# The third pair's k and q loaded earlier and transposed by DMA from ScalarE's queue, in a fused retention and bilinear-FFN kernel

## The chip, the cores and the metric

The kernel runs on one core of a Trainium2 chip. The metric is the device time of one execution in microseconds. The five engines of a core run their own instruction queues: TensorE (PE, with weight loads shown apart as PEld), VectorE (DVE), ScalarE (ACT), GpSimd (POOL), and SyncE (SP), which here only issues transfers. Sixteen DMA engines move the data.

## The reference

Inputs are q, k, v of shape (4, 8, 768, 64), that is batch, heads, sequence and head size, and three weights w_a, w_b (512 x 1536) and w_out (1536 x 512). All of them are float32.

```python
for t in range(S):                       # per batch and head, gamma = 1 - 2^(-5-h)
    state = gamma * state + outer(k[t], v[t])
    y[t] = scale * q[t] @ state
x = y.transpose(0, 2, 1, 3).reshape(B * S, H * D)     # 3072 tokens x 512
out = ((x @ w_a) * (x @ w_b)) @ w_out
```

## The kernel before, in words

The sequence is cut into 24 chunks of 128 rows, called slots 0 to 23, six for each batch entry. The recurrence is computed by chunks: inside a chunk by a masked matrix of scores k.q, between chunks by a running state. The decay is folded into k and q when they are scaled by a table and turned to bf16 (`scaled`, line 212; the result is `kqb`, with k and q side by side).

The FFN works on token tiles; `TILES` says how many slots each of the eight tiles has. The first tile has four slots (512 tokens). For each of twelve blocks `ft` of 128 hidden columns, `ffn_a` (line 504) makes `a` with four matmuls, which ScalarE copies to bf16 (line 508), and `ffn_g` (line 516) makes `g`, which VectorE multiplies with that copy (line 519). `parts` splits a block's matmuls into two halves of columns where it says so. When all twelve blocks are done, `ffn_out` (line 544) multiplies by w_out.

Slots 0 to 5 go by pairs (a pair `u` is slots 2u and 2u+1, loaded by `load_pair` in one transfer each for k, q and v). Their k and q have to be transposed before the scores: `flip2` does that on TensorE against an identity (line 395), into PSUM, and ScalarE or VectorE copies the result to SBUF (`kT2`, `qT2`). Pairs 0 and 1 run at the start, since they feed the first FFN tile; pair 2, the third one, is worked in between the blocks of the first tile. From slot 6 on, `casts` scales a slot on POOL and transposes it with a DMA that SP issues (`dma_start_transpose`, line 225); `turn` later runs its states and scores.

The order of work is written out by hand. `seq` chains every instruction of an engine to the one before it, so each engine runs in the order in which the code is written. `LOADS` is the order of SP's first transfers: k, q, v by pair, `w0` to `w5` (a sixth of w_a and of w_b each), `o0` to `o5` (w_out) and `s6`, `s7` (the loads of slots 6 and 7). POOL turns weights to bf16 (`cast_w`, `cast_o`, line 184). Blocks 2j and 2j+1 use the weights of `w`j.

Around the change the written order of TensorE is: blocks 2 to 7 in pairs (a, a, g, g), block 8, the transposes of the third pair's k, a of block 9, the transposes of its q, g of block 9, the scores of both slots (`scores2`, line 408), the first state update (`update2`, line 431), a of blocks 10 and 11, g of block 10, `intra2` and `inter2` (lines 460 and 448), g of block 11, the second tile's twelve blocks, and then the output matmuls, with `turn(6, None)` ahead of the second output row block and `turn(8, 6)` some 11 us later. PSUM has three rotating banks for `a`, `g`, `tp` and half of the scores (pool `psff`); the staging buffers of weights rotate by four, so `o4` and `o5` reuse those of `w4`.

Of the kernel before, what the change touches and what calls it, by code (L numbers as in the profile page):

```python
# [10 lines left out]
BF16 = mybir.dt.bfloat16  # L11
# [5 lines left out]
PAIRS = 3  # L17


LOADS = "k0 q0 k1 q1 v0 v1 w0 w1 w2 w3 w4 k2 q2 v2 w5 o0 o1 o2 o3 o4 o5 s6 s7".split()  # L20


@with_exitstack
def kernel(
# [10 lines left out]
    nc = tc.nc  # L35
    P = 128
    B, H, S, D = q.shape
    NCH = S // P
    HP = H // 2
# [3 lines left out]
    NFT = DFF // P  # L43
    NSLOT = B * NCH
    NW = 6
    WC = DFF // NW
    FPW = NFT // NW
# [11 lines left out]
    tra = ctx.enter_context(tc.tile_pool(name="tra", bufs=4))  # L59
# [22 lines left out]
    def load_slot(t, names="kqv"):  # L82
        b, ci = divmod(t, NCH)
        for nm in names:
            if t % 2 == 0:
                whole[nm] = raw.tile([P, 2, H, D], F32, tag=nm + "f", name=nm + "f")
            raws[nm, t] = whole[nm][:, t % 2]
            s = {"k": k, "q": q, "v": v}[nm][b, :, ci * P : (ci + 1) * P, :]
            seq(nc.sync.dma_start(out=raws[nm, t], in_=s.rearrange("h p d -> p h d")))
# [21 lines left out]

    pending = list(LOADS)

# [9 lines left out]
    kqb = {}  # L123
# [52 lines left out]
    wa_bf = wpool.tile([P, KT, DFF], BF16, name="wa_bf")  # L176
    wb_bf = wpool.tile([P, KT, DFF], BF16, name="wb_bf")
    wo_bf = wpool.tile([P, NFT, DM], BF16, name="wo_bf")

    def cast(engine, dst, src):  # L180
        if engine is nc.scalar:
            seq(nc.scalar.copy(dst, src))  # L182
        else:
            seq(engine.tensor_copy(dst, src))  # L184

    def cast_w(j, parts=1):
        for nm, dst in (("a", wa_bf), ("b", wb_bf)):
            for x in range(parts):
                a, b = x * WC // parts, (x + 1) * WC // parts
                cast(nc.gpsimd, dst[:, :, j * WC + a : j * WC + b], wst[nm, j][:, :, a:b])  # L190
# [15 lines left out]
    def scaled(eng, t, i):  # L206
        ktab, qtab = tabs[0] if t < 2 * PAIRS else tabs[1]
        dst, src, tab = kqb[t][:, i], raws["kq"[i], t], (ktab, qtab)[i][:, t % NCH]
        dst = dst.rearrange("p hp r d -> p r hp d")
        src = src.rearrange("p (r hp) d -> p r hp d", r=2)  # L210
        tab = tab.rearrange("p (r hp) o -> p r hp o", r=2).to_broadcast([P, 2, HP, D])
        seq(eng.tensor_tensor(dst, src, tab, op=ALU.mult))  # L212

    def new_nat(t):
        kqb[t] = nat.tile([P, 2, HP, 2, D], BF16, tag="kqb", name="kqb")
        kb[t], qb[t] = kqb[t][:, 0], kqb[t][:, 1]
        vb[t] = nat.tile([P, H, D], BF16, tag="vb", name="vb")

    def casts(t, names="kqv"):
        if "k" in names:  # L220
            new_nat(t)
            scaled(nc.gpsimd, t, 0)
            scaled(nc.gpsimd, t, 1)
            kqT[t] = tra.tile([P, 2, HP, P], BF16, tag="kqT", name="kqT", bufs=6)
            seq(nc.sync.dma_start_transpose(
                out=kqT[t].rearrange("p a b c -> p (a b) c"),
                in_=kqb[t].rearrange("p a hp r d -> p (a hp r d)")))
            if t % 2 and t + 1 < NSLOT:
                for names in ("kq", "v"):
                    load_slot(t + 1, names)  # L230
                    load_slot(t + 2, names)
        if "v" in names:
            cast(nc.gpsimd, vb[t], raws["v", t])

    def half(i):
        return slice(64 * i, 64 * i + 64)
# [52 lines left out]

    ys, begun = {}, set()  # L290

    after = mybir.DependencyInfo(mybir.DependencyClass.Sync, mybir.DependencyReason.DATA)
    mark = lgr[:, 0, :1]
    fence = {}

# [75 lines left out]
                later.append(lambda c=c: leave(old, c, apart))  # L371


    kT2, qT2, ats = {}, {}, {}
# [12 lines left out]
    def flip2(u, i, on):  # L387
        into = (kT2, qT2)[i]
        if u not in into:
            into[u] = tra.tile([P, 2, HP, P], BF16, tag="kq"[i] + "T2", name="kq"[i] + "T2", bufs=2)  # L390
        for pars, eng in on:
            tp = psff.tile([P, 2, HP, P], BF16, tag="ff", name="tp")[:, : len(pars)]
            for m, par in enumerate(pars):
                for hp in range(HP):
                    seq(nc.tensor.transpose(tp[:, m, hp, :], kqb[2 * u + par][:, i, hp, :, :], ident))  # L395
            cast(eng, into[u][:, pars[0] : pars[0] + len(pars)], tp)

    def scores2(u, par, ff=False):
        t = 2 * u + par
# [21 lines left out]
    def update2(u, c, keep=True):  # L421
        if (u, c) == (PAIRS - 1, 1):
            return
        if (u, c) == (0, 0):
            state[0] = psst.tile([P, HP, D], F32, tag="st", name="st")
        st = state[0]
        for par in range(2):
            for hp in range(HP):
                for r in range(2):
                    t = 2 * u + par  # L430
                    seq(nc.tensor.matmul(st[half(r), hp, :], kb[t][half(c), hp, r, :],  # L431
                                         vb[t][half(c), HP * r + hp, :],
                                         start=((u, c, hp, par) == (0, 0, 0, 0)),
                                         stop=(hp == HP - 1), skip_group_check=True))
        if keep:
            keep_state(c)
# [52 lines left out]

    def parts(J, ft, c0, c1):  # L490

        if J == 0 and ft in (2, 3):
            return [(c0, (c0 + c1) // 2), ((c0 + c1) // 2, c1)]
        return [(c0, c1)]

    def ffn_a(J, ft, c0=0, c1=None):
        c1 = TILES[J] * P if c1 is None else c1
        if J not in ht:
            ht[J] = htp.tile([P, NFT, 4 * P], BF16, tag="ht", name="ht")
        fs = slice(ft * P, (ft + 1) * P)  # L500
        a = psff.tile([P, 4 * P], F32, tag="ff", name="a")[:, : c1 - c0]
        for kt in range(KT):
            for b0, b1 in parts(J, ft, c0, c1):
                seq(nc.tensor.matmul(a[:, b0 - c0 : b1 - c0], wa_bf[:, kt, fs], xcols(J, kt, b0, b1),  # L504
                                     start=(kt == 0 and b0 == c0), stop=(kt == KT - 1 and b1 == c1),
                                     skip_group_check=True))
        asb = asbs[J, ft, c0] = asbp.tile([P, 4 * P], BF16, tag="asb", name="asb")[:, : c1 - c0]
        seq(nc.scalar.copy(asb, a))  # L508

    def ffn_g(J, ft, c0=0, c1=None):  # L510
        c1 = TILES[J] * P if c1 is None else c1
        fs = slice(ft * P, (ft + 1) * P)
        g = psff.tile([P, 4 * P], F32, tag="ff", name="g")[:, : c1 - c0]
        for kt in range(KT):
            for b0, b1 in parts(J, ft, c0, c1):
                seq(nc.tensor.matmul(g[:, b0 - c0 : b1 - c0], wb_bf[:, kt, fs], xcols(J, kt, b0, b1),  # L516
                                     start=(kt == 0 and b0 == c0), stop=(kt == KT - 1 and b1 == c1),
                                     skip_group_check=True))
        seq(nc.vector.tensor_tensor(ht[J][:, ft, c0:c1], g, asbs.pop((J, ft, c0)), op=ALU.mult))  # L519

    def ffn_ab(J, ft):
        store()
        ffn_a(J, ft)
        ffn_g(J, ft)
        catch_up(2)
# [30 lines left out]
    D_, G_, A_ = nc.vector, nc.gpsimd, nc.scalar  # L556
    K, Q, V = 0, 1, 2
# [46 lines left out]
    ffn_g(0, 0, W2, 2 * W2)  # L604
    ffn_g(0, 1, W2, 2 * W2)
    keep_state(1)
    for ft in range(2, NFT):
        if ft % FPW == 0 and ft // FPW + 1 < NW - 1:
            cast_w(ft // FPW + 1)
        if ft == 7:  # L610
            casts2(2, {(i, par): G_ for i in (K, Q, V) for par in range(2)})
            cast_w(NW - 1)
        if ft < 8 and ft % 2 == 0:
            ffn_a(0, ft)
            ffn_a(0, ft + 1)
# [12 lines left out]
    update2(2, 0)  # L628
    ffn_a(0, 10)
    ffn_a(0, 11)  # L630
    ffn_g(0, 10)
# [72 lines left out]
```

## Time and profile before

| what | value |
|---|---|
| median of 3 runs | 226.66 us (226.16 to 226.73) |
| profiled execution, its own time | 226.44 us |
| its span (first to last instruction) | 224.7 us |
| busy share of the span | PE 97%, DVE 43%, ACT 43%, POOL 36% |
| granted TensorE clock | 1.000 |
| transferred | 39.72 MB, 177 GB/s over the span |

In a timeline row come the start in us, the duration in us, the engine, the line, the operation, what is written from what, and how many of them; in square brackets stands the idle time ahead of it and what ended that. In the chain of waits each row is a start, a duration and whose time it is. A row of windows has the stretch, its length, then the busy time of PE, PEld, DVE, ACT and POOL with their number of instructions, the granted clock, the DMA engines' share and GB/s. The sizes of transfers are followed by the time from issue to landing.

### The profile page before, as it was taken

The page shows a single profiled execution, that of the slowest core. Times are in us where ns is not written, and L with a number is a line of the kernel's source. Part 1 is how long each engine was busy: PE and PEld are TensorE (multiplying, and loading weights), DVE is VectorE, ACT ScalarE, POOL GpSimd, SP SyncE. Part 2 cuts the span into 40 slices and gives each one's busy share as a digit, 9 for nine tenths or more (in the row PEclk, how much of TensorE's full clock was granted, in tenths as well). Part 3 has the DMA queues.
Part 4 walks back from the last instruction along what each step waited for, and adds up shares of the span by engine and source line. Part 5 has one row for each costly group of instructions (what it writes and reads, how often), then busy time and mean ns, then how long its engine had stood idle before and what let it go on. Part 6 is the DMA issues. An engine that isn't in the chain of part 4 may idle for free.

```text
span 224.7 us, 6284 instructions
## 1 busy us (share of the span) xinstructions
PE 217.7 (97%) x2632; PEld 132.3 (59%) x2632; DVE 96.2 (43%) x195; ACT 96.0 (43%) x206; POOL 80.3 (36%) x105
## 2 busy tenths in 40 slices
PE   7789999999999999999999999999999999999994
PEld 7568645786456866876875444554444544444443
DVE  3784347553415435472466343544343522333300
ACT  3465335342427436454457333355433354333221
POOL 5577798781534435352625235350000000000000
PEclk9999999999999999999999999999999999999999
DMA  6999999998899996999979996974100012100022
GB/s 180 347 379 382 365 303 401 297 210 176 208 222 241 250 228 136 208 233 192 213 174 230 110 267 169 251 125 143 47 0 0 3 50 93 47 3 1 0 93 95
DMA packets 96124, 39.72 MB, mean 177 GB/s; under 512 B 76000, under 2 KB 91616, under 8 KB 96096
## 3 DMA queue, kind: packets, MB, share of 16 engines
q1 hardware_dynamic: 95952, 39.20, 67.8%
q8 instruction: 20, 0.33, 0.6%
q10 hardware_dynamic: 144, 0.13, 0.2%
q14 instruction: 8, 0.07, 0.1%
HBM read 28.31 MB, written 6.29 MB: 154 GB/s over the span
## 4 chain that ended last, share of the span: by engine, by line
PE 92%; DMA 3%; ACT 1%; POOL 1%; issue 1%; SPq 0%; POOLq 0%
PE o L544 28%; PE g L516 28%; PE a L504 28%; DMA kf<-in_k_dram 3%; PE y L321 1%; POOL kqb L212 1%; PE at L280 1%; PE y L333 1%; PE st L257 1%; PE y L460 1%; PE y L448 1%; PE tp L395 0%; PE st L431 0%; SPq L95 0%; ACT qT L182 0%
## 5 line engine op out<-in xcount | busy, mean ns | idle before, releaser
L519 DVE TENSOR_TENSOR ht<-g,asb 128x256 bf16<-128x256 f32 (+1 forms) x98 | 53.9, 550 | 84.6 <-PE g L516 74.6
L516 PE MATMUL g<-xt,wb_bf 128*128 128x256 bf16 (+1 forms) x400 | 77.7, 319 | 0.1
L504 PE MATMUL a<-xt,wa_bf 128*128 128x256 bf16 (+1 forms) x400 | 77.7, 319 | 0.0
L508 ACT CAST asb<-a 128x256 bf16<-128x256 f32 (+1 forms) x98 | 46.3, 472 | 71.2 <-PE a L504 71.0
L544 PE MATMUL o<-wo_bf,ht 128*128 128x512 bf16 (+2 forms) x312 | 64.4, 363 | 0.0
L504 PEld LDWEIGHTS <-wa_bf 128*128 128x128 bf16 x400 | 38.8, 98 | 24.0 <-DVE xt L184 0.4
L516 PEld LDWEIGHTS <-wb_bf 128*128 128x128 bf16 x400 | 39.1, 98 | 23.1 <-issue 0.2
L544 PEld LDWEIGHTS <-ht 128*128 128x128 bf16 x312 | 28.8, 98 | 30.6
L212 POOL TENSOR_TENSOR kqb<-kf,ktab 128x512 bf16<-128x512 f32 x22 | 22.8, 1042 | 40.9 <-DMA kf<-in_k_dram 36.2
L182 ACT COPY osb<-o 128x512 f32<-128x512 f32 (+2 forms) x25 | 14.1, 564 | 33.1 <-PE o L544 25.0
L212 POOL TENSOR_TENSOR kqb<-qf,qtab 128x512 bf16<-128x512 f32 x21 | 22.3, 1063 | 1.1 <-DMA qf<-in_q_dram 1.1
L184 POOL CAST vb<-vf 128x512 bf16<-128x512 f32 x25 | 14.9, 610 | 20.0 <-DMA vf<-in_v_dram 13.0
L182 ACT CAST gst<-sums 128x256 bf16<-128x256 f32 x33 | 13.4, 405 | 6.4 <-DVE sums L271 3.1
L271 DVE TENSOR_TENSOR sums<-st,sums 128x256 f32<-128x256 f32 x30 | 12.7, 424 | 1.9 <-PE st L257 0.4
L286 DVE TENSOR_TENSOR aT<-at,mask 128x512 bf16<-128x512 f32 x18 | 11.5, 681 | 0.0
L344 ACT CAST xt<-y 128x512 bf16<-128x512 f32 x16 | 8.5, 583 | 0.0
L483 PE MATMUL idle<-zero 128*128 128x170 bf16 (+1 forms) x56 | 7.2, 294 | 1.1 <-DVE zero L126 1.1
L418 DVE TENSOR_TENSOR aT<-at,mask 128x512 bf16<-128x512 f32 x12 | 7.4, 681 | 0.7 <-PE at L408 0.7
L184 POOL CAST wa_bf<-wsta 128x1024 bf16<-128x1024 f32 (+1 forms) x7 | 6.4, 918 | 2.8 <-DMA wsta<-in_moe_w_a_dram 2.6
L184 POOL CAST wo_bf<-wsto 128x1024 bf16<-128x1024 f32 x6 | 6.2, 1040 | 2.1 <-DMA wsto<-in_moe_w_out_dram 2.1
L184 POOL CAST wb_bf<-wstb 128x1024 bf16<-128x1024 f32 (+1 forms) x7 | 6.4, 918 | 1.6 <-DMA wstb<-in_moe_w_b_dram 1.6
L298 DVE COPY lgr<-bq 128x1 f32<-128x1 f32 x4 | 0.6, 154 | 14.2 <-PE y L321 14.2
(53 smaller groups left out, 91.5 us busy)
## 6 DMA issues: line engine op xcount, KB each, us to landing
out_dram<-osb SPq DMA_DIRECT2D x23, 256.0 KB, 2.6
kf<-in_k_dram SPq DMA_DIRECT2D x18, 256.0 KB, 4.3
qf<-in_q_dram SPq DMA_DIRECT2D x18, 256.0 KB, 4.3
vf<-in_v_dram SPq DMA_DIRECT2D x18, 256.0 KB, 4.5
wsta<-in_moe_w_a_dram SPq DMA_DIRECT2D x6, 512.0 KB, 7.7
wstb<-in_moe_w_b_dram SPq DMA_DIRECT2D x6, 512.0 KB, 7.7
wsto<-in_moe_w_out_dram SPq DMA_DIRECT2D x6, 512.0 KB, 8.4
kf<-in_k_dram SPq DMA_DIRECT2D x3, 512.0 KB, 5.8
```

The costliest lines, as they stand in the source:

```text
L182: seq(nc.scalar.copy(dst, src))
L184: seq(engine.tensor_copy(dst, src))
L212: seq(eng.tensor_tensor(dst, src, tab, op=ALU.mult))
L271: seq(nc.vector.tensor_tensor(new, u[c][:, s], old, op=ALU.add))
L286: seq(nc.vector.tensor_tensor(aT[n][:, r].rearrange("p s h d -> p (s h) d"), at[:, r].rearrange("p s h d -> p (s h) d"), mask.to_broadcast ...
L344: seq(nc.scalar.copy(dst, ys[o][c]))
L418: seq(nc.vector.tensor_tensor(aT[t][:, r], ats[t][r], masks[par].to_broadcast([P, HP, P]), op=ALU.mult))
L504: seq(nc.tensor.matmul(a[:, b0 - c0 : b1 - c0], wa_bf[:, kt, fs], xcols(J, kt, b0, b1), start=(kt == 0 and b0 == c0), stop=(kt == KT - 1 a ...
L508: seq(nc.scalar.copy(asb, a))
L516: seq(nc.tensor.matmul(g[:, b0 - c0 : b1 - c0], wb_bf[:, kt, fs], xcols(J, kt, b0, b1), start=(kt == 0 and b0 == c0), stop=(kt == KT - 1 a ...
L519: seq(nc.vector.tensor_tensor(ht[J][:, ft, c0:c1], g, asbs.pop((J, ft, c0)), op=ALU.mult))
L544: seq(nc.tensor.matmul(o, ht[J][:, ft, i * P : (i + 1) * P], wo_bf[:, ft, c0:c1], start=(ft == 0), stop=(ft == NFT - 1)))
```

## The change

`LOADS` has k2 and q2 ahead of w4 instead of behind it. POOL's casts of the third pair move ahead of, and in between, those of w4. The transposes of the third pair's k and q on TensorE and their three copies are gone; two DMA transposes, issued by ScalarE behind its copy of block 7, write one tile `T2` instead, a slot each. The scores stay behind block 9, which now follows block 8 directly. The first DMA transpose that SP issues later (slot 6) waits for TensorE's first state update of the third pair. Blocks 4 and 5 of the first tile are split into halves as blocks 2 and 3 were: four groups (a and g of each) of eight matmuls over 256 columns instead of four over 512.

```diff
-LOADS = "k0 q0 k1 q1 v0 v1 w0 w1 w2 w3 w4 k2 q2 v2 w5 o0 o1 o2 o3 o4 o5 s6 s7".split()
+LOADS = "k0 q0 k1 q1 v0 v1 w0 w1 w2 w3 k2 q2 w4 v2 w5 o0 o1 o2 o3 o4 o5 s6 s7".split()
...
-    def cast_w(j, parts=1):
-        for nm, dst in (("a", wa_bf), ("b", wb_bf)):
+    def cast_w(j, parts=1, names="ab"):
+        for nm in names:
+            dst = wa_bf if nm == "a" else wb_bf
...
+    queues_apart = {}
...
-            seq(nc.sync.dma_start_transpose(
+            bi = seq(nc.sync.dma_start_transpose(
                 out=kqT[t].rearrange("p a b c -> p (a b) c"),
                 in_=kqb[t].rearrange("p a hp r d -> p (a hp r d)")))
+            if queues_apart:
+                tc.add_manual_dep(bi.ins, queues_apart.pop(0), after, reason="one queue transposes")
...
+    def flip_by_dma(par):
+        u = PAIRS - 1
+        if u not in kT2:
+            both = tra.tile([P, 2, 2, HP, P], BF16, tag="T2", name="T2", bufs=1)
+            kT2[u], qT2[u], flipped[0] = both[:, :, 0], both[:, :, 1], both
+        seq(nc.scalar.dma_start_transpose(
+            out=flipped[0][:, par].rearrange("p a b c -> p (a b) c"),
+            in_=kqb[2 * u + par].rearrange("p a hp r d -> p (a hp r d)")))
...
-        if J == 0 and ft in (2, 3):
+        if J == 0 and ft in (2, 3, 4, 5):
...
-    for ft in range(2, NFT):
-        if ft % FPW == 0 and ft // FPW + 1 < NW - 1:
+    for ft in range(2, 8, 2):
+        if ft < 6:
             cast_w(ft // FPW + 1)
-        if ft == 7:
-            casts2(2, {(i, par): G_ for i in (K, Q, V) for par in range(2)})
+        else:
+            casts2(2, {(K, 0): G_, (K, 1): G_, (Q, 0): G_})
+            cast_w(4, names="a")
+            casts2(2, {(Q, 1): G_})
+            cast_w(4, names="b")
+            casts2(2, {(V, 0): G_, (V, 1): G_})
             cast_w(NW - 1)
-        if ft < 8 and ft % 2 == 0:
-            ffn_a(0, ft)
-            ffn_a(0, ft + 1)
-            ffn_g(0, ft)
-            ffn_g(0, ft + 1)
-        if ft == 8:
-            ffn_ab(0, ft)
-    flip2(2, K, [((0, 1), A_)])
+        ffn_a(0, ft)
+        ffn_a(0, ft + 1)
+        if ft == 6:
+            flip_by_dma(0)
+            flip_by_dma(1)
+        ffn_g(0, ft)
+        ffn_g(0, ft + 1)
+    ffn_a(0, 8)
+    ffn_g(0, 8)
     ffn_a(0, 9)
-    flip2(2, Q, [((0,), D_), ((1,), D_)])
     ffn_g(0, 9)
     scores2(2, 0, True)
     mask2(2, 0)
     scores2(2, 1)
     mask2(2, 1)
     update2(2, 0)
+    queues_apart[0] = last[mybir.EngineType.PE].name
```

More of the change, by code (lines that the diff above doesn't have):

```diff
@@ L217, in new_nat @@
         vb[t] = nat.tile([P, H, D], BF16, tag="vb", name="vb")
+    queues_apart = {}
+    after = mybir.DependencyInfo(mybir.DependencyClass.Sync, mybir.DependencyReason.DATA)
     def casts(t, names="kqv"):
@@ L290 @@
     ys, begun = {}, set()
-    after = mybir.DependencyInfo(mybir.DependencyClass.Sync, mybir.DependencyReason.DATA)
     mark = lgr[:, 0, :1]
@@ L371, in turn @@
                 later.append(lambda c=c: leave(old, c, apart))
-    kT2, qT2, ats = {}, {}, {}
+    kT2, qT2, ats, flipped = {}, {}, {}, {}
     def casts2(u, on):
```

## The prediction

> **What bounds the kernel now.** I read the chain that ended last, first summed by engine, then in order of time around the third pair.
>
> ```profile
> PE 92%; DMA 3%; ACT 1%; POOL 1%; issue 1%; SPq 0%; POOLq 0%
> ...
> 21.16 1.75 PE a L504 x16
> ...
> 24.66 1.73 PE a L504 x8
> ...
> 31.56 0.86 PE a L504 x4
> 32.43 0.86 PE g L516 x4
> 33.29 0.46 PE tp L395 x8
> 33.80 0.89 issue
> 34.68 0.60 ACT asb L508
> 35.33 1.02 PE g L516 x4
> 36.35 0.57 PE at L408 x32
> ...
> 37.20 1.89 PE a L504 x8
> 39.09 0.86 PE g L516 x4
> ```
>
> TensorE is the bound: 92% of the chain, and every other stretch is its own time or a hole in it. The one hole after the start lies here. Block 8 ends at 33.29, the scores begin at 36.35: 3.06 us for what are two groups of 0.86 (a and g of block 9) and the transposes of k (0.46) and q. The g of block 9 begins only at 35.33, behind the "issue" and ScalarE's copy of 34.68.
>
> Next the timelines of POOL and, in the last row, ScalarE.
>
> ```profile
> 25.97 1.04 POOL L184 CAST wa_bf<-wsta 128x1024 bf16<-128x1024 f32 x1 [0.37 <-DMA wsta<-in_moe_w_a_dram]
> 27.33 1.04 POOL L184 CAST wb_bf<-wstb 128x1024 bf16<-128x1024 f32 x1 [0.32 <-DMA wstb<-in_moe_w_b_dram]
> 28.84 2.04 POOL L212 TENSOR_TENSOR kqb<-kf,ktab 128x512 bf16<-128x512 f32 x2 [0.47 <-DMA kf<-in_k_dram]
> 30.84 2.04 POOL L212 TENSOR_TENSOR kqb<-qf,qtab 128x512 bf16<-128x512 f32 x2
> 32.82 1.17 POOL L184 CAST vb<-vf 128x512 bf16<-128x512 f32 x2
> 33.93 1.04 POOL L184 CAST wa_bf<-wsta 128x1024 bf16<-128x1024 f32 x1
> 35.25 1.04 POOL L184 CAST wb_bf<-wstb 128x1024 bf16<-128x1024 f32 x1 [0.28 <-DMA wstb<-in_moe_w_b_dram]
> ...
> 29.87 0.58 ACT L508 CAST asb<-a 128x512 bf16<-128x512 f32 x1 [0.28 <-PE a L504]
> ```
>
> POOL runs at the heels of SP's transfers: w4's halves land at 25.9 and 27.3, k2 at 28.8, and the second half of w5 at 35.2.
>
> **The change part by part.** *TensorE.* From 33.29 to the a of block 10 at 37.20 pass 3.91 us. Without transposes and hole there are a and g of block 9 (2 x 0.86), the scores (0.57) and the update (what is left of 36.35 to 37.20, 0.28): 2.57. That saves 1.34. The halves cost 1.75 − 1.73 for two blocks' a, and the same for g: 0.04. If everything arrives in time, TensorE is 1.30 ahead at block 10. Block 8 no longer passes `store` and `catch_up`, which hold nothing there yet. The copies that go (one on ScalarE, two on VectorE) save nothing of their own.
>
> *Loads and POOL.* k2 takes w4's place: it lands at about 26.0, q2 at 27.5, w4 at 28.9 and 30.2; v2 and w5, behind the same bytes as before, stay. k2 and q2 have the third buffer and wait for nothing in SP's queue. On POOL with 1.02 a scaling and 1.04 a weight cast: K, K, Q from 26.05 to 29.1; w4's first half to 30.15; Q to 31.2; its second half to 32.2; V to 33.4; then w5 at its landing, 33.9. Block 8 is to begin at 31.60 (31.56 + 0.04) and needs the first half: 1.4 to spare. Its g, at 32.47, needs the second: 0.3 to spare. I take 0; if both loads are 0.3 later, TensorE waits 0.3, a fifth of the gain. o5 reuses that half's staging, its issue comes after 33, so SP doesn't wait.
>
> *The transposes on ScalarE.* The trace has this instruction on SP only.
>
> ```profile
> L225 SPq DMA_TRANSPOSE kqT<-kqb x18: 1232/1296/2036, 46.6 to 151.9; - x18
> ...
> DMA to landing us min/median/max: 2.7/3.6/6.1
> ```
>
> Issuing took 1.23 to 2.04 us, and ScalarE does nothing else in that time. At 1.25 (the median is nearest to an undisturbed queue): the first from 30.45, when block 7's copy ends (29.87 + 0.58), to 31.70; the second, whose Q was ready at 31.2, to 32.95. Queued behind them is block 8's copy, ready at 32.5, now 32.95 to 33.55. Its bank is wanted again by g of block 9 at 34.2, so 0.65 is spare: cost 0. VectorE's product of block 8 slips to 33.55–34.25, ahead of the scores, which want its bank at 35.06. At 2.04 each the copy would end at 35.1 and g wait 0.9.
>
> Landing, counted from issue, took 2.7 to 6.1. For the second transpose, issued at 31.70, that is 34.4 to 37.8; at the median 35.3. The scores need both slots' q, so the second decides, and they could begin at 35.06. Hence cost 0 to 2.7; I take the median, 0.25, leaving 1.05 gained.
>
> *What the transposes do to SP's transfers.* Below are three stretches of windows, then the packets of three stretches: 138.4–139.9 (nothing but one DMA transpose), 32.0–33.5 (w5) and 35.5–40.2 (w_out).
>
> ```profile
> 31.00:32.00 1.00, 1.00 (x6) 0.46 (x5) 0.83 (x2) 0.00 (x0) 1.00 (x2) 1.00 0.96 313
> 33.00:34.00 1.00, 1.00 (x12) 0.65 (x11) 0.60 (x1) 0.28 (x2) 1.00 (x3) 1.00 1.02 348
> 36.00:38.00 2.00, 1.97 (x54) 1.26 (x53) 1.54 (x3) 0.73 (x2) 1.54 (x3) 1.00 1.05 406
> 138.75:139.00 0.25, 0.25 (x3) 0.10 (x1) 0.00 (x0) 0.00 (x0) 0.00 (x0) 1.00 1.29 293
> ...
> DMA packets 1056, 0.26 MB, mean 175 GB/s; under 512 B 1056, under 2 KB 1056, under 8 KB 1056
> ...
> DMA packets 507, 0.51 MB, mean 340 GB/s; under 512 B 16, under 2 KB 500, under 8 KB 507
> ...
> DMA packets 985, 1.93 MB, mean 411 GB/s; under 512 B 53, under 2 KB 53, under 8 KB 983
> ```
>
> One transpose moves 0.26 MB at 293 GB/s: 0.9 us of all engines, 1.8 for both. From 31 to 34 the engines moved 313 to 348 where they can do 406, so up to half a microsecond of that fits into gaps. SP's transfers behind it are late by 0 (all in gaps) to 1.8; I take 1.3.
>
> The Trainium skill (DMA: Bandwidth & Descriptors, "Issuing engines are not separate DMA queues") says that transfers from ScalarE and SP run on the same engines, and a second issuer saves only issue time. By that rule the delay is the full 1.8, and the sum below would give a gain of about 0.1. The gaps in the windows speak for a little less.
>
> Late first is w5. Its first half lands at 33.9 + 1.3 = 35.2, is cast by 36.2, and block 10 wants it at 35.9: 0.3 lost, 0.25 of which the late landing takes anyway. Its second half lands at 36.5, is cast by 37.6, wanted at 38.0: free. So TensorE is some 1.0 ahead at block 10. The w_out casts have microseconds to spare. Then come slots 6 to 9, whose transposes SP issues. Rows: k of slot 7 (issue, landing, POOL's scaling), slot 7's transpose with its landing and the scores of slots 6 and 7, slot 9's transpose with its landing and the scores of slots 8 and 9.
>
> ```profile
> 43.38 0.80 SPq L89 DMA_DIRECT2D kf<-in_k_dram  x1
> ...
> kf<-in_k_dram SPq DMA_DIRECT2D x1, 256.0 KB, 4.4
> ...
> 48.27 1.04 POOL L212 TENSOR_TENSOR kqb<-kf,ktab 128x512 bf16<-128x512 f32 x1 [1.10 <-DVE ht L519]
> ...
> 50.34 1.23 SPq L225 DMA_TRANSPOSE kqT<-kqb  x1
> ...
> DMA to landing us min/median/max: 3.2/3.2/3.2
> ...
> 55.47 0.49 PE L280 MATMUL at<-kqT 64*64 64x64 bf16 x32
> ...
> 62.38 1.31 SPq L225 DMA_TRANSPOSE kqT<-kqb  x1
> ...
> DMA to landing us min/median/max: 3.0/3.0/3.0
> ...
> 66.81 0.45 PE L280 MATMUL at<-kqT 64*64 64x64 bf16 x32
> ```
>
> Slot 7's transpose lands at 53.5, 1.9 before its scores; slot 9's at 65.4, only 1.4 before. In SP's queue slot 9's transpose stands behind slot 7's and the loads between. Whatever TensorE gains plus whatever SP's chain loses must stay under 1.4, or TensorE waits at slot 9's scores. k of slot 7 landed at 47.8 and POOL took it at 48.27, so about 0.5 of SP's 1.3 is free and 0.8 reaches the transposes. At slots 6 and 7, 1.0 + 0.8 is under 1.9. At slots 8 and 9, 1.4 − 0.8 leaves 0.6 of gain. With a delay of 1.8 it leaves 0.1, with none it takes nothing away.
>
> *The new wait* on slot 6's transpose is for an instruction of about 36 us; behind it stand SP's later loads, but SP comes to it after 46: cost 0. If the third pair were 10 us late, it would hold SP.
>
> **Sum.** 1.30 − 0.25 (landing) − 0.05 (w5 beyond that) − 0.4 (slot 9) = 0.6 faster: 226.44 − 0.6 = 225.8. The profiled execution, 226.44, lies 0.22 under the median of the runs, which is noise here; 0.3%, 0.68 us, is about what a measurement of this kernel can tell from no change.
>
> **The rivals.** *All the gain stays.* If the transposes go into gaps, SP's chain is not late, slot 9's slack of 1.4 holds the 1.30, and landing in 3.3 or less keeps it: 225.2. For it: 2.7 was seen, 313 GB/s leaves room. Against it: w_out follows at 406, without gaps.
>
> *The second transpose lands late.* At 6.1, the longest seen, it lands at 37.8; the scores begin 1.45 after the 36.35 of before, so 227.9. From a landing 4.65 after issue on (36.35) the change is no longer a gain. For it: the landings of 6.1 and SP's backlog at that time. Against it: the median of 3.6.
>
> *The queues take turns, packet by packet.* This is the rival that goes farthest to the other side. A transpose is 1056 packets, about 64 an engine beside the closing ones. w5's packets take 1.5 us / (507/16) = 47 ns, w_out's 4.7 / (985/16) = 76 ns, the transpose's own 0.9 us / 64 = 14 ns. If each waits for one of SP's, the first transpose takes 64 x 61 ns = 3.9 us, from 31.7 to 35.6, and the second, beside w_out, 64 x 90 = 5.8, to 41.4. The scores then begin 5.1 late: 231.5. It decides where both are through only after 36.35: 4.65 us for 128 turns of 14 ns and one of SP's, so from 22 ns a packet of SP's on. For it: the packets are of such unequal size. Against it: the trace has no stretch with two loaded queues. The Trainium skill (DMA: Bandwidth & Descriptors, "Queues, rings and completion order") states this rule, a round of turns at packet granularity, where a packet can hold several descriptors; no run so far shows how many.
>
> **How the numbers follow.** The forecast (slot 9 takes part of the gain back) has 0.46, its own range 225.4 to 226.4: 0.18 below 225.76, 0.28 within. All the gain: 0.18. Landing late: 0.20. Turns: 0.16. Faster 0.36, same 0.28, slower 0.36. The range goes from 225.2 (all the gain) to 228.0 (the longest landing); turns are left out, with some of the tails.
>
> **What would show it.** Right: no line 395 after 30 us; two DMA transposes in ScalarE's queue near 30.5 and 31.7, issued in 1.2 to 1.3 each; scores at 35.1 to 35.6, block 10 near 36.2; w_out's casts about 1.3 later; slot 9's scores with a wait on a DMA, near 66.2. Wrong: TensorE idle before line 408 beyond 36.4; g of block 8 waiting for POOL; g of block 9 for ScalarE; slot 9's scores without a wait.

## The result and the profile after

The changed kernel takes 237.76 us (median of 5 runs, 237.61 to 238.25) against 226.66 (226.16 to 226.88) for the kernel before in the same session. The ratio is 1.0502, with a 95% interval of 1.0487 to 1.0518: 11.1 us slower, where 0.6 faster was forecast. The profiled execution took 237.76, its span is 236.0.

First the chain of waits of the changed kernel around the third pair (start, duration, whose time).

```profile
29.50 2.69 DMA wsto<-in_moe_w_out_dram
32.19 13.24 DMA T<-kqb
45.44 0.14 issue
45.57 1.07 PE at L422 x28
46.64 0.42 PE st L445 x16
47.06 3.24 PE a L518 x8
50.30 0.86 PE g L530 x4
```

TensorE no longer carries this stretch. One DMA transpose does, for 13.24 us. The scores (now line 422) begin at 45.57 instead of 36.35, so 9.22 late. From there to g of block 10 the kernel before needed 2.74 (36.35 to 39.09), the changed one 4.73 (45.57 to 50.30): 1.99 more. Together that is 11.21, and the spans differ by 11.3, so the whole loss arises between 30 and 50 us.

The two transposes, from the view of their line in that stretch (durations of issuing, then the time from issue to landing):

```profile
L408 ACTq DMA_TRANSPOSE T<-kqb x2: 1392/3720/6047, 30.7 to 32.2; - x2
DMA to landing us min/median/max: 11.1/12.2/13.2
```

Issuing took 1.39 and 6.05 us, and they landed at 30.67 + 11.1 = 41.8 and 32.19 + 13.2 = 45.4. ScalarE and TensorE in the timeline:

```profile
30.67 7.57 ACTq L408 DMA_TRANSPOSE T<-kqb  x2
38.34 1.07 ACT L522 CAST asb<-a 128x512 bf16<-128x512 f32 x2 [7.87 <-POOL wo_bf L184]
...
38.97 1.86 PE L530 MATMUL g<-xt,wb_bf 128*128 128x512 bf16 x4 [4.81 <-ACT asb L522]
45.57 1.07 PE L422 MATMUL at<-T 64*64 64x128 bf16 x32 [4.73 <-DMA T<-kqb]
```

TensorE stands idle twice: 4.81 us in front of g of block 9, because ScalarE could not copy block 8 while it was issuing, and 4.73 us in front of the scores. The windows of these stretches (stretch, length, busy time of PE, PEld, DVE, ACT, POOL, granted clock, DMA share, GB/s):

```profile
30.00:35.00 5.00, 4.16 (x20) 1.76 (x18) 1.39 (x2) 0.47 (x1) 4.43 (x7) 1.00 1.06 362
35.00:40.00 5.00, 1.03 (x3) 0.40 (x3) 0.69 (x1) 1.07 (x2) 3.23 (x4) 0.62 1.08 376
40.00:45.00 5.00, 0.84 (x2) 0.00 (x0) 0.69 (x1) 0.00 (x0) 3.53 (x4) 0.50 1.17 312
45.00:50.00 5.00, 4.43 (x56) 2.51 (x57) 2.48 (x4) 1.32 (x3) 4.05 (x5) 0.51 1.13 254
```

During the idle time the granted clock falls to half, and it is still at 0.51 while the scores and the a of blocks 10 and 11 run; those eight matmuls take 3.24 us instead of 1.89. The Trainium skill (TensorE: Matmul & The Clock Gate, "Part 1: The HAM clock gate") says that the clock goes to half after an idle window of about 3.4 us. The trace agrees that it goes to half, but not on the length: the last matmul ahead of the first hole ends at 34.17, and windows of 0.25 us show the clock at half from 36.2 on, some 2 us later. In a run below it falls behind an idle time of 2.40 us.

Last the DMA queues (q1 is SyncE's, q10 ScalarE's: packets, MB, share of 16 engines), before the first turn of the transposes and while the first of them runs, 30.7 to 35.0 and 35.0 to 41.2:

```profile
q1 hardware_dynamic: 1445, 1.59, 105.6%
q10 hardware_dynamic: 26, 0.01, 0.7%
...
q1 hardware_dynamic: 1079, 2.08, 89.8%
q10 hardware_dynamic: 1066, 0.27, 19.1%
```

Up to 35.0, three microseconds after its issue had ended (32.06), next to nothing of the first transpose has moved: 26 packets of 1056. Then the two queues move packets in equal number, 1079 to 1066. SyncE's carry 2 KB (the w_out loads), ScalarE's 256 bytes. One turn takes 6.2 us / (1066 / 16 engines) = 93 ns, where a transpose alone had 14 ns a packet. Later, from 42.0 to 44.5, when SyncE's queue carries loads of slots and most of its packets are under 512 bytes, the numbers are still equal, 801 to 803, and a turn takes 2.5 us / (803 / 16) = 50 ns. In this trace, then, the size of the neighbour's packets sets the pace, as the third rival has it.

### The profile page after: what moved, and what is told of

Same layout as the page of the kernel before. It is cut to its first block, busy times and chain, and to the rows that moved or that the text cites. A ratio compares the mean times of both kernels' runs of the same rounds, so it can differ in the third digit from the quotient of the medians.

```text
span 236.0 us, 6284 instructions
## 1 busy us (share of the span) xinstructions
PE 219.9 (93%) x2632; PEld 134.4 (57%) x2632; DVE 95.4 (40%) x193; ACT 95.0 (40%) x205; POOL 80.5 (34%) x105
## 4 chain that ended last, share of the span: by engine, by line
PE 79%; DMA 10%; SPq 7%; POOL 1%; issue 0%; DVE 0%; ACT 0%
PE o L558 27%; PE a L518 24%; PE g L530 23%; DMA T<-kqb 6%; SPq L103 4%; DMA kf<-in_k_dram 3%; SPq L95 3%; PE y L326 1%; POOL kqb L213 1%; PE at L286 1%; PE y L338 1%; DMA wsto<-in_moe_w_out_dram 1%; PE st L263 1%; PE at L422 0%; PE y L474 0%
## 5 line engine op out<-in xcount | busy, mean ns | idle before, releaser
L530 PE MATMUL g<-xt,wb_bf 128*128 128x256 bf16 (+1 forms) x408 | 78.5, 319 | 4.8 <-ACT asb L522 4.8
L518 PE MATMUL a<-xt,wa_bf 128*128 128x256 bf16 (+1 forms) x408 | 79.1, 321 | 0.1
L530 PEld LDWEIGHTS <-wb_bf 128*128 128x128 bf16 x408 | 40.0, 98 | 27.8 <-issue 5.9
L518 PEld LDWEIGHTS <-wa_bf 128*128 128x128 bf16 x408 | 39.9, 99 | 24.6 <-issue 2.1
L213 POOL TENSOR_TENSOR kqb<-kf,ktab 128x512 bf16<-128x512 f32 x22 | 22.9, 1043 | 50.0 <-DMA kf<-in_k_dram 45.2
L497 PE MATMUL idle<-zero 128*128 128x170 bf16 (+1 forms) x56 | 7.7, 310 | 1.1 <-DVE zero L126 1.1
L497 PEld LDWEIGHTS <-zero 128*128 128x128 bf16 x56 | 6.5, 126 | 1.3 <-DVE zero L126 1.1
L454 ACT CAST gbd<-st 64x256 bf16<-64x256 f32 x10 | 3.7, 365 | 8.4 <-PE st L445 8.3
```

Of the source, the lines that this page charges most:

```text
L497: seq(nc.tensor.matmul(idle[:, :w], zero[:, :P], zero[:, :w], start=True, stop=True, skip_group_check=True))
```

## The experiments

Ratios are to the kernel before, measured on the same chip in the same session. Theory A is that of the third rival: the two queues take turns, so a transpose in ScalarE's queue goes at the pace of SyncE's large packets. Its opponents are named in the expectations.

### Without the backlog

The w_out loads and all later ones wait for the first state update of the third pair, so that the transposes have the DMA engines to themselves; nothing else differs from the changed kernel.

```diff
-        seq(nc.sync.dma_start(out=st, in_=s))          # load_o
+        bi = seq(nc.sync.dma_start(out=st, in_=s))
+        if held_loads:
+            tc.add_manual_dep(bi.ins, held_loads.pop(0), after, reason="held back")
...
-    issue_loads(100)
+    issue_loads(5)
...
+    queues_apart[0] = held_loads[0] = last[mybir.EngineType.PE].name
+    issue_loads(100)
```

> The changed kernel, with SP's six w_out transfers and all later loads held until TensorE's first state update of the third pair. Theory A (turns: on each DMA engine a packet of ScalarE's transpose waits for one packet of SP's, so SP's backlog sets the landing): only w5 is left to share with, both transposes land by 37.0 to 37.5, ScalarE's second issue ends by 36, the scores begin near 37.5, no granted clock below 1; w_out and the loads of slots 6 to 9 then come some 3 us late, and slots 6 to 9 wait for them: 228 to 230 us. Theory B (a transpose that ScalarE issues is slow of itself, 11 to 13 us): the landing stays near 45 and the time at 237 to 238. If the first packets of the transposes still come only near 35, three microseconds after the issue, the late start is not made by the w_out transfers.

Measured: 230.24 us (2 runs), ratio 1.017 (1.0124 to 1.0216). Landing of the transposes, and TensorE's rows:

```profile
DMA to landing us min/median/max: 4.9/5.2/5.4
...
35.30 1.02 PE L534 MATMUL g<-xt,wb_bf 128*128 128x512 bf16 x4 [0.84 <-ACT asb L526]
36.73 0.64 PE L426 MATMUL at<-T 64*64 64x128 bf16 x32 [0.40 <-DMA T<-kqb]
```

The same transposes at the same place now land in 4.9 and 5.4 us instead of 11.1 and 13.2, and of the 9.22 us by which the scores were late 0.38 remain. What slows a transpose is the traffic beside it, not ScalarE. Its first packets come at 33.0 instead of just before 35.0, 1.4 us behind the end of the first issue (31.60), so part of the late start too is made by the w_out transfers. The time, 0.2 over the expected range, stays 3.7 us above the kernel before, and the held loads are seen in the trace: POOL waits 5.67 us for w_out and casts it from 41.48 on, and TensorE later waits 1.5 us for the transpose of slot 7.

### Loads and POOL order of the change, transposes on TensorE

```diff
-        if J == 0 and ft in (2, 3, 4, 5):
+        if J == 0 and ft in (2, 3):
...
-            flip_by_dma(0)
-            flip_by_dma(1)
...
+    flip2(2, K, [((0, 1), A_)])
     ffn_a(0, 9)
+    flip2(2, Q, [((0,), D_), ((1,), D_)])
```

> The changed kernel with the third pair's transposes back on TensorE, where they were before, and blocks 4 and 5 whole again; the earlier k2 and q2 and POOL's new order stay. Theory A: all of the loss belongs to the DMA transposes, so 226.0 to 226.8, with the hole at block 9 about as long as before, since copies and banks make it, not the late k and q. Rival D (w4 behind k2 and q2 is part of the loss): block 8 or its g waits for POOL, over 227. If the hole came from the late casts of q, up to 0.5 faster than before.

Measured: 226.33 us (10 runs) against 226.52, ratio 0.9992 (0.9976 to 1.0008): no difference. The earlier k2 and q2 and the new order on POOL cost nothing and bring nothing by themselves. The whole loss belongs to the DMA transposes, and to the halves that went out with them, which a run below takes alone.

### The transposes in SyncE's queue

Two places: ahead of w5's loads, and behind them.

```diff
-        seq(nc.scalar.dma_start_transpose(
+        seq(nc.sync.dma_start_transpose(
...
-    issue_loads(100)
+    issue_loads(4)          # ahead of w5 (behind it: 5); the rest follows both transposes
```

> The changed kernel with the two transposes issued by SyncE, in the order of its own queue, between v2 and w5; everything else as in the changed kernel. Theory A (the loss is the turns that two queues take, and a blocked ScalarE): in one queue there are no turns; the first goes out when POOL's cast of k and the second when that of q is done (28 and 31 us), each takes about 1 us of transfer and lands some 3 us behind its issue, at 34 to 35.5, before the scores' place at 35.1; w5 goes out some 2 us later and its two casts with it. Scores 35 to 36, the clock at full, 225 to 227.5. Theory B (DMA transposes of this size are slow wherever they are issued, 5 us and more each): landings past 40, 232 and more.

> As the run with SyncE's transposes, but behind w5 instead of ahead of it. Theory A: the transposes' packets come behind w5's (all gone at about 35) and ahead of all of w_out's; landings 36.5 to 38, scores 36.5 to 38 instead of 45.57, 226.5 to 229. Theory B (slow wherever issued): landings past 42, 234 and more. Between this and the run ahead of w5 stands the price of one load of 0.5 MB ahead in the queue, some 1.5 to 2.5 us.

Measured: ahead of w5 228.55 us (5 runs), ratio 1.0074 (1.0052 to 1.0096); behind it 227.63 (10 runs, 226.51 to 229.46), ratio 1.0059 (1.003 to 1.0088). Ahead of w5, the landing and TensorE:

```profile
DMA to landing us min/median/max: 2.8/3.3/3.8
...
35.24 0.64 PE L422 MATMUL at<-T 64*64 64x128 bf16 x32
37.71 1.90 PE L518 MATMUL a<-xt,wa_bf 128*128 128x512 bf16 x8 [1.57 <-POOL wa_bf L184]
```

In a single queue the transposes do just what the forecast had them do on ScalarE: 2.8 and 3.8 us to land, scores at 35.24 without a wait. But what stands behind them in the queue is now late: block 10 waits 1.57 us for the cast of w5, and slot 7's scores later wait 1.6 us for their own transpose. Behind w5 the landings take 4.5 and 6.4 us, and it is the third pair's scores that wait:

```profile
36.65 0.64 PE L422 MATMUL at<-T 64*64 64x128 bf16 x32 [1.58 <-DMA T<-kqb]
```

So 1.6 us of waiting is handed from one place to the other. The time in the first order came out 1 us over the expected range, in the second within it.

### The transposes behind w5, and v last

The run before showed w5 and v2 in front of the transposes. Here w5 goes out before v2, v2 behind the transposes, its cast behind w5's, and the state update, which needs v, behind block 11's a.

```diff
-LOADS = "... k2 q2 w4 v2 w5 o0 ...".split()
+LOADS = "... k2 q2 w4 w5 v2 o0 ...".split()
...
-    update2(2, 0)
     ffn_a(0, 10)
     ffn_a(0, 11)
+    update2(2, 0)
```

> The run with both transposes in SyncE's queue behind w5, and in it w5 loaded ahead of the third pair's v, v behind the transposes, its cast behind w5's and the state update of the third pair behind block 11's a (it needs v). It asks whether the scores' lateness in that run (36.65 instead of the 35.1 of a landing in time) is only w5's transfer ahead in the same queue. Theory A (in one queue a transpose costs its own transfer and lands some 3 us behind its issue): w5 is out of the way 1.5 us sooner, landings at 35 to 35.7, scores at 35.1 to 36, 225.6 to 226.6. Theory B (the transposes themselves are late beside a full queue): scores at 36.5 or later, 226.8 to 228.5.

Measured: 227.80 us (6 runs), ratio 1.0062 (1.0041 to 1.0084). TensorE:

```profile
35.42 0.64 PE L422 MATMUL at<-T 64*64 64x128 bf16 x32 [0.28 <-DMA T<-kqb]
36.00 1.90 PE L518 MATMUL a<-xt,wa_bf 128*128 128x512 bf16 x8
38.71 0.31 PE L445 MATMUL st<-vb,kqb 64*64 64x64 bf16 x8 [0.81 <-POOL vb L184]
```

The place of the scores came as theory A had it: they begin at 35.42, 1.23 earlier than in the run before and 0.93 earlier than in the kernel before. The time did not, 1.2 over the expected range: v, cast at 38.04, takes 0.81 + 0.25 us, and the transposes of slots 7 and 9 another 0.16 and 0.39. Whichever transfer was put last in these three orders was the one that was missed.

### Smaller packets beside the transposes

Other slot loads first: the loads of slots 6 and 7 (256-byte packets) go out ahead of w_out's (2 KB), so that small packets stand beside the transposes.

```diff
-LOADS = "... w5 o0 o1 o2 o3 o4 o5 s6 s7".split()
+LOADS = "... w5 s6 s7 o0 o1 o2 o3 o4 o5".split()
```

> The changed kernel with the order of two groups of loads exchanged: the slot loads of steps 6 and 7 (256-byte packets) go out behind w5 and ahead of the six w_out loads (2 KB packets). The two transposes stay in ScalarE's queue, at the same place and behind the same transfers. Theory A (the two queues take turns, one packet each on every DMA engine, so each packet of a transpose waits for one packet of SyncE's queue): in the changed kernel 64 packets per engine of one transpose took 5.9 us beside 2 KB packets, some 92 ns a turn; beside 256-byte packets (14 ns each by the transposes' own rows) a turn is some 28 ns and a transpose 1.8 us, so the landings come at 38 to 40.5 instead of 41.8 and 45.4, the scores at 39 to 41 instead of 45.57, and the whole takes 229 to 232. Theory B (a transpose is slow in ScalarE's queue whatever stands beside it): landings at 42 and 45 as before, 237 to 238. Later w_out loads cost at most what they are late: 1 us in the casts, which had 0.3 us and more to spare.

Measured: 233.68 us (2 runs), ratio 1.0311 (1.0262 to 1.0359). Landing, and the scores:

```profile
DMA to landing us min/median/max: 6.5/7.1/7.7
...
40.40 1.07 PE L422 MATMUL at<-T 64*64 64x128 bf16 x32 [2.54 <-DMA T<-kqb]
```

The landings move to 37.6 and 40.3 and the scores to 40.40, near the range of theory A (38 to 40.5, and 39 to 41); the time is 1.7 over its upper end, with the clock at 0.50 in 40 to 45 us here too, although the two idle times of TensorE were only 2.65 and 2.54 us. But the reason that theory A gave, one small packet for each of the transpose's, is not what the queues show. This is 38 to 39 us:

```profile
q10 hardware_dynamic: 715, 0.18, 81.9%
q1 hardware_dynamic: 409, 0.10, 45.9%
```

From 37.75 to 38.5 the counts are 794 to 46, and from 36.0 to 36.5 they are 385 to 22: the transposes moved for long stretches with next to nothing of SyncE's beside them. So of the 9.22 us by which the scores were late, 5.17 go when w_out's 2 KB packets are not beside the transposes. What small packets in equal number would cost, this run does not show; why SyncE's were so few is open, since its load of slot 7's k was issued by 36.96 and landed only at 40.9.

The same was tried by cutting each w_out load in two, with 1 KB packets.

```diff
-        seq(nc.sync.dma_start(out=st, in_=s))
+        for x in range(2):
+            h = slice(x * DM // 2, (x + 1) * DM // 2)
+            seq(nc.sync.dma_start(out=st[:, :, h], in_=s[:, :, h]))
```

> The changed kernel with each w_out transfer cut into two by columns, so that its packets are 1 KB instead of 2 KB; all else is the same. Theory A: 64 turns of 42 to 47 plus 14 ns are 3.6 to 3.9 us a transpose beside w_out instead of 5.8; ScalarE's second issue ends some 2 us earlier, near 36, the second landing near 42 instead of 45.4, the time 234 to 235. Theory B, or a fixed share of the bytes for each queue: no change, 237.8.

Measured: 238.82 us (2 runs), ratio 1.0549 (1.0508 to 1.059): missed. With twice as many transfers the wait in front of ScalarE's first transpose ended only at 34.48 instead of 30.67. From issue to landing it was 8.9 and 10.4 us instead of 11.1 and 13.2, but the later start takes more than that. Equal counts are not there either (552 of the transposes to 50 of SyncE's from 42 to 43). The run changed two things and decides nothing.

### A plain copy in ScalarE's queue

The kernel before, with a copy of 256 KB within SBUF issued by ScalarE where the changed kernel issues its first transpose.

```diff
+            if ft == 6:
+                spare = const.tile([P, 2, HP, 2, D], BF16, name="spare")
+                seq(nc.scalar.dma_start(out=spare, in_=kqb[0]))
```

> The kernel before, with one plain copy of 256 KB within SBUF (the cast k and q, 2 KB packets, eight per engine) issued by ScalarE at about 30.5, where the changed kernel issues its first transpose; nobody reads it. It asks how long a second queue waits for its first turn, without any transpose. Theory A (the wait for the first turn is one of the queue, whatever it carries): first packet 2 to 3.5 us behind the issue, while SyncE's w_out is under way, and then turns one for one, done some 1.5 us later. Theory B (it is the transpose): first packet within 1 us. The copy costs the rest at most its 256 KB of bandwidth, about 1 us of w_out, and 226 to 227.5.

Measured: 226.43 us (8 runs), ratio 1.0003 (0.999 to 1.0015). The queues in 30.9 to 35.0, then in 35.1 to 37.5, and the copy's issue with its time to landing:

```profile
q1 hardware_dynamic: 1107, 1.16, 91.8%
q10 hardware_dynamic: 2, 0.00, 0.3%
...
q1 hardware_dynamic: 379, 0.72, 77.7%
q10 hardware_dynamic: 140, 0.25, 27.5%
...
spare<-kqb ACTq DMA_DIRECT2D x1, 256.0 KB, 7.5
```

The copy was issued at 30.30 in 0.52 us, and up to 35.0 two of its packets had moved: more than four microseconds of waiting for the first turn, with no transpose in it. In the changed kernel, too, the first turn came just before 35.0. So the wait belongs to the second queue and not to the transpose; that it lasts until the transfers SyncE has already handed over are through fits both runs, and is inferred. It was longer than the 2 to 3.5 expected. The other half of the expectation, turns one for one and an end 1.5 us later, is not borne out: the copy landed at 37.8, 2.8 behind 35.0, and the counts are 140 to 379.

### The second transpose later

The second transpose is issued behind ScalarE's copies of blocks 8 and 9 instead of ahead of them.

```diff
             flip_by_dma(0)
-            flip_by_dma(1)
...
     ffn_a(0, 9)
+    flip_by_dma(1)
```

> The changed kernel with the second transpose issued behind ScalarE's copies of block 9 instead of ahead of block 8's. It asks whether ScalarE's blocked queue (6.05 us for the second issue, g of block 9 4.81 us late) costs anything of its own. Theory A (what counts is the landing of the second transpose, and its packets get their turns only behind the first's): the copy of block 8 comes at 33.5 instead of 38.34, g of block 9 at 35, and the second transpose, issued at about 36, still lands at 44.5 to 46.5; 236.5 to 239. Theory B (a blocked ScalarE is the loss): the scores come with the first landing, near 42, and the time falls by 3 us or more.

Measured: 237.63 us (2 runs), ratio 1.0485 (1.0452 to 1.0518). Landing, and the scores:

```profile
DMA to landing us min/median/max: 8.8/9.9/11.1
...
45.30 1.07 PE L422 MATMUL at<-T 64*64 64x128 bf16 x32 [9.98 <-DMA T<-kqb]
```

Issued at 36.41 instead of 32.19 it lands at 45.2 all the same. ScalarE is free and block 9 comes at once, and nothing is won: instead of 4.81 and 4.73 us, TensorE now idles 9.98 us in front of the scores. ScalarE's blocked queue costs nothing of its own. In this run the two queues again move equal numbers of packets (178 to 186 from 38 to 39).

### What the clock costs

82 idle matmuls of 256 columns in the two holes were to keep the clock up.

```diff
+            warm(42, psat, "y1")        # ahead of g of block 9
     ffn_g(0, 9)
+    warm(40, psat, "y1")
```

> The changed kernel with idle matmuls on zeros in TensorE's two holes: 42 ahead of g of block 9 and 40 ahead of the third pair's scores. Theory C (about 2.0 of the 11.1 us come from the granted clock, which falls to half in the holes and slows the scores, the update and a of blocks 10 and 11): the clock stays at 1, the scores still begin near 45.5, the time is 235.5 to 236. If the half clock costs nothing, 237.8 or a little more.

Measured: 239.01 us (2 runs), ratio 1.0558 (1.0527 to 1.0588). The scores came at 46.99, 1.4 later than in the changed kernel, with an idle time of 2.40 in front of them, and a of blocks 10 and 11 still took 3.39 us. The cover was too short, so it does not price the clock. It shows something else: these 2.40 us were enough for the clock to be at 0.50 from 48.1 to 51.4, while holes of 1.57 and 1.58 us in the runs with SyncE's transposes left it at 1.00. With 54 longer matmuls, and blocks 4 and 5 whole:

```diff
-        if J == 0 and ft in (2, 3, 4, 5):
+        if J == 0 and ft in (2, 3):
...
+    hold(22)                    # idle matmuls of 512 columns
     ffn_g(0, 9)
+    hold(32)
```

> The changed kernel with blocks 4 and 5 whole (16 matmuls fewer) and 54 idle matmuls of 512 columns (0.216 us each at full clock) in the two holes, 22 ahead of g of block 9 and 32 ahead of the scores; they keep TensorE busy up to the landing of the transposes. It asks what the fall of the granted clock to 0.5 costs. If the clock is the reason for the 2.0 us by which the way from the scores to g of block 10 grew (2.74 before, 4.73 changed), that way is 2.7 to 3.0 here, and the time 235.5 to 236.5. If it is something else, the way stays at 4.5 or more and the time at 237.5 to 238.5.

Measured: 237.53 us (2 runs), ratio 1.0489 (1.0464 to 1.0515).

```profile
47.14 0.57 PE at L422 x32
47.96 1.83 PE a L524 x8
49.79 0.86 PE g L536 x4
```

From the scores to g of block 10 it is 2.65 us, as in the kernel before, at a granted clock of 1.00 throughout. So the 1.99 us there are the clock's. The time falls by 0.2 only: the idle matmuls themselves end 1.57 later than the scores began in the changed kernel, and behind g of block 10 another 0.8 us is lost (236.3 − 49.79 against 236.0 − 50.30), where the chain has a stop of TensorE of 0.79 at 131.13 for which the next two runs give a likely reason. The expected 235.5 to 236.5 was missed.

### The halves

The kernel before with blocks 4 and 5 in halves, and, to see whether it is the halves, the kernel before with 16 idle matmuls of 16 columns instead.

```diff
-        if J == 0 and ft in (2, 3):
+        if J == 0 and ft in (2, 3, 4, 5):
```

> The kernel before, with blocks 4 and 5 of the first tile in halves as blocks 2 and 3 are (16 matmuls more, nothing else). Expected 0.04 us more, so no difference that can be measured: 226.3 to 227.0. Rival: the halves cost 16 fixed parts of a matmul, 16 x 0.02 to 0.06 us, 0.3 to 1.0 us in all: 227 to 227.6.

```diff
+            if ft == 4:         # behind g of block 5
+                for _ in range(16):
+                    seq(nc.tensor.matmul(idle[:, :16], zero[:, :P], zero[:, :16], start=True, ...))
```

> The kernel before with 16 idle matmuls of 16 columns behind block 5 of the first tile and all blocks as they were; it asks why the halves of blocks 4 and 5 alone cost 1.8 us (226.43 to 228.25), where block 9 comes no later than before. Theory R (TensorE fetches its instructions in pieces of a fixed count; 16 more of them anywhere move every later fetch, and one then falls where TensorE runs through short matmuls, 1.1 us of idling inside the attention of a slot step at 99.29 in the profile with halves): 16 others do the same, 227.8 to 228.6 here with an idle time near 99 to 100. Theory H (the halves themselves cost it): only the 16 idle matmuls' own 0.3 us or less, 226.4 to 226.9.

Measured: halves 228.25 us (6 runs), ratio 1.0074 (1.005 to 1.0097); sixteen others 228.18 (5 runs), ratio 1.0065 (1.0045 to 1.0085). Their chains and that of the kernel before, at the same place in a slot's attention some 70 us further on, in the order halves, sixteen others, before:

```profile
98.96 0.33 PE y L333 x30
99.29 1.11 issue
100.40 0.22 PE y L333 x2
```

```profile
99.48 0.43 PE y L333 x30
99.91 1.42 issue
```

```profile
99.08 0.35 PE y L333 x32
99.43 5.29 PE o L544 x24
```

With halves block 9 ends no later than before (36.34 against 36.35), so the halves themselves are free. Both runs then stop TensorE behind the 30th of 32 short matmuls, for 1.11 and 1.42 us, waiting for nothing that the profile shows; the kernel before runs through. Sixteen instructions of another kind stop it at the same place, so it is not the halves as such; what the two runs share is the number. The sixteen themselves take 0.43 us (scores at 36.71 against 36.28 in the timelines), and the profile is that of the slowest of the five executions, 229.51, with a second stop of 0.68 at 124.67. That the stop is a wait for instructions fits and is inferred; no row names it. A packet of the instruction queue (q8) passes 1 to 2 us ahead of each of the three stops, at 97.8, 98.8 and 122.6, but one passes at 99.2 in the kernel before, too, with no stop behind it. The Trainium skill (Runtime: NRT & Kernel Launch, "Instruction fetch mechanics") has instructions fetched in blocks of 256 and calls crossing a block mostly hidden. Here 16 instructions more cost 1.7 to 1.8 us, and no run shows the crossing itself.

In the changed kernel the 16 matmuls of the halves take the place of the 16 transposes that went, so the count behind them is that of before (2632 in both profiles), and no such stop is in its chain.

### Transposes on TensorE, k's earlier

With k and q cast earlier, k's transposes can go ahead of g of block 8 and q's behind it, so that the copies lie beside other work.

```diff
     ffn_a(0, 8)
+    flip2(2, K, [((0, 1), A_)])
     ffn_g(0, 8)
+    flip2(2, Q, [((0, 1), D_)])
     ffn_a(0, 9)
```

> The earlier loads of the changed kernel with the transposes back on TensorE, as in the run that was level with the kernel before, but K's ahead of g of block 8 and Q's behind it, so that the copy of K out of PSUM lies beside g of block 8. If the hole before the scores (0.46 us in the kernel before) is the wait for those copies, it goes: 226.0 to 226.3 against 226.5. If it is something else, or if the transposes now wait for the cast of Q, no gain: 226.4 to 227.

Measured: 226.47 us (12 runs) against 226.43, ratio 1.0002 (0.9993 to 1.0011).

```profile
35.78 0.64 PE L422 MATMUL at<-qT,kT 64*64 64x128 bf16 x32
36.25 0.42 PE L445 MATMUL st<-vb,kqb 64*64 64x64 bf16 x16
36.70 1.67 PE L518 MATMUL a<-xt,wa_bf 128*128 128x512 bf16 x7
```

The hole goes: block 10 begins at 36.70 instead of 37.20, and TensorE is still 0.50 ahead at 80.48 (80.98 before). But at the output matmuls of 116.43 (116.46 before) the lead is gone, in part through a wait for VectorE's product at 112.62. TensorE's last output matmuls begin 0.43 earlier than in the kernel before (210.75 against 211.18), but in the run with the transposes where they were, and the hole still there, they do so 0.37 earlier (210.81), so that is not the hole's. The time shows neither. No version tried beats the kernel before.

## Why the prediction was wrong

*The step that failed: the landing of the transposes.* The forecast took the time from issue to landing from SyncE's transposes (2.7 to 6.1) and chose the median of 3.6, a cost of 0.25. It was 11.1 and 13.2 us. Those rows came from a time with one loaded queue; what they did not hold was a second one. The same transposes in SyncE's queue landed in 2.8 and 3.8 us, with the scores at 35.24, so the number was right for the queue it was read from, with no load ahead; behind w5 in that queue it was 4.5 and 6.4.

*The rival of the turns had the mechanism and missed the size.* Its price of a turn beside w_out (76 + 14 = 90 ns) was measured as 93, and its break-even of 22 ns a packet of SyncE's was far exceeded. It gave 231.5 because it let the first turn come at 31.70; it came just before 35.0, some three microseconds behind the end of its issue, and the plain copy shows such a wait without any transpose. So the first transpose, too, had 2 KB packets for neighbours and not w5's. That is 41.4 forecast against 45.4 measured for the second landing. And it had no clock in it: 1.99 us. A 0.16 for this rival was too little: the one reason given against it, that no stretch of the trace had two loaded queues, was a reason not to know, not one against. With w_out coming at 406 GB/s without a gap behind w5, as the windows showed, two loaded queues were certain. The Trainium skill (DMA: Bandwidth & Descriptors, "Queues, rings and completion order") states turns between queues by packets, and equal counts of 1079 and 1066 agree; how many go in one turn, the counts don't show. In the two runs with smaller packets the counts were not equal (409 to 715, 50 to 552), so how far this mechanism reaches is open.

*ScalarE.* Expected were two issues of 1.25 us and block 8's copy 0.65 ahead of its need; the first took 1.39, the second 6.05. The copy was 38.34 instead of 32.95, and g of block 9 waited for ScalarE, as the list of signs for a wrong forecast had it. It goes with packets that don't move: with the backlog held back the second issue took 2.88, and issued later, while the first transpose's packets moved, 1.51. It was no loss of its own, by the run with the second transpose later.

*TensorE's gain of 1.30.* Never reached in the changed kernel. With SyncE issuing ahead of w5 the scores did begin at 35.24, within 0.2 of the forecast's 35.06. The halves at 0.04 were right up to block 9, but alone they cost 1.8 through a stop far behind it, which the sum had no term for; that the changed kernel was spared it, since 16 other instructions went, was luck.

*POOL's order and the earlier loads, taken at 0:* right. With the transposes on TensorE, the same loads and casts are level with the kernel before (0.9992).

*Transfers late behind the transposes, 1.3 us of SyncE's, and slot 9's scores as the next wait:* not testable where the third pair is 11 us late; slot 9's scores had no wait. In the runs with SyncE's transposes the next late thing was w5 (1.57) and slot 7's transpose (1.6); slot 9's scores did wait, for 0.39, in the run with v last. The forecast let w5 be 1.3 late at a price of 0.05; the transposes ahead of it made it late enough to cost 1.57, and those behind it cost the scores 1.58. That they have to stand ahead of or behind something in a busy stretch was the price not seen.

## What to carry to other kernels

A small transfer that something waits for does not belong in a second queue beside a stream of large packets: here it first waited some 3 us, and then went at the other queue's pace, packet for packet, at 93 ns beside 2 KB packets where alone it had 14. In the stream's own queue it landed in 2.8 to 6.4 us, and then the question is which transfer behind it is missed first. When TensorE idles for more than 2 us or so, reckon with the slow clock behind the idle time (2.40 brought it here, 1.58 did not); and when the number of its instructions changes, look for a stop in short matmuls far behind the change.

## What the runs showed that was not expected

- A second queue's first turn came just under 3 us (transpose) and over 4 us (plain copy) behind the end of its issue, with SyncE's queue full, and 1.4 with the w_out loads held back.
- Issuing on ScalarE can block it for 6.05 us, where the packets of its own earlier transfer hardly moved; where they moved, it took 1.51.
- The granted clock fell to 0.50 some 2 us into an idle time of 4.81 and cost 1.99 us in the 4.7 us from the scores on; in other runs holes of 2.40, and of 2.65 and 2.54 in a row, brought it to 0.50.
- Sixteen short matmuls cost 1.7 us, 0.43 of it their own; the profile has stops of 1.42 us some 70 us behind them and of 0.68 at 124.67. The same number taken out and put in costs nothing.
- A 256 KB copy in a second queue beside everything else cost nothing (1.0003), as long as nobody waited for it.
